# Moving the first batch's v from GpSimd's DMA queue to SyncE's in a fused attention and MLP-mixer kernel

## The chip, the cores and the metric

One core of a Trainium2 chip. The metric is device time in microseconds (us) of one execution; a profile of one execution gives the span. Where runs are timed in rounds, the kernel before runs on the same chip in the same rounds.

## The reference

```python
# q, k, v: (8 batches, 8 heads, 576, 64) float32; s: (8, 8, 576)
scores = scale * q @ k.T                       # causal
bias   = -(cum[:, :, :, None] - cum[:, :, None, :])   # cum = cumsum(max(s, 0))
attn   = softmax(where(causal, -1e9, scores + minimum(bias, 0)))
x      = (attn @ v) with the heads side by side          # (8, 576, 512)
u      = x + (relu(x.T @ w_tok1) @ w_tok2).T              # token mixing
out    = u + relu(u @ w_ch1) @ w_ch2                      # channel mixing
```

## The kernel before

A planner in the kernel simulates the engines with fixed durations and writes one static order of instructions for each engine, and that order is the program. k, q and the weights are cast to bf16 while loading, on GpSimd's queue. v stays float32. In the first batch its loads stand on GpSimd's queue too, between and behind k and q and ahead of the weights:

```python
def load(c=c, n=n, p0=p0):                     # chunk c of v: 128 positions, 8 heads
    (nc.sync if b >= 2 else nc.gpsimd).dma_start(
        out=vf.t[p0 : p0 + n, c, :, :],
        in_=v[b, :, c * 128 : c * 128 + n, :].rearrange("h p d -> p h d"))   # rows of 64 float32
...
# then on VectorE, chunk by chunk: vp = vf * wT   (all products with v need all five chunks)
...
sv = stage_v(0)
stage_qk(0, 0)                # first k and q
stage_qk(0, 1, (0,))          # second k
load_consts(); weights()
next(sv)                      # v, chunk 0
stage_qk(0, 1, (1,))          # second q
run(sv)                       # v, chunks 1 to 4
load_tok()                    # w1, w2, then wc1, v of batch 1, its k and q, wc2
```

Of k or q one load covers four of the eight heads, called a quad: 128 rows, each 4608 bytes of float32 read and 2304 of bf16 written. In idle stretches of the start the planner puts "unread matmuls" of zeros on TensorE to keep its clock up.

## Time and profile before

| | before |
|---|---|
| median of 5 runs | 288.22 us (287.94 to 288.91) |
| span of the profiled run | 289.3 us |
| TensorE busy | 278.7 us, 96% |
| last chunk of the first v multiplied, starts at | 19.48 us |
| first channel matmul (start of the dense part) | 28.7 us |

### The profile page before, as it was taken

To read this page: it belongs to the slowest core of one execution; us is meant where nothing else is said; L and a number is where in the kernel's file an instruction comes from. 1 tells how busy PE (TensorE), PEld (TensorE's weight loads), DVE (VectorE), ACT (ScalarE), POOL (GpSimd) and SP (SyncE) were. 2 spreads that over 40 slices of the span, in tenths; PEclk is the share of its full clock that TensorE was granted. 3 is DMA by queue.
4 is the path that set the end of the run, shared out by engine and by line. 5 is a ranking of instruction groups with operands and counts; after the bars stand their busy time and mean duration, and the time that the engine had idled before them with its cause. 6 is when DMAs were issued, how large, how long until landed. Compare 5 with 4: busy or idle time off the path is not lost.

```text
span 289.3 us, 6464 instructions
## 1 busy us (share of the span) xinstructions
PE 278.7 (96%) x2556; PEld 160.2 (55%) x2587; DVE 191.8 (66%) x425; ACT 169.2 (59%) x288; POOL 46.3 (16%) x97
## 2 busy tenths in 40 slices
PE   7799999999999999998999999999999999999994
PEld 2357866656664554455764454546764454457643
DVE  7756857899998998997986399889145360530022
ACT  4474787999975758744962269864770256107600
POOL 8775610121202021001100022200000000000000
PEclk9879999999999999999999999999999999999999
DMA  6999999999593999699383446893004410260032
GB/s 122 234 217 248 224 210 213 220 214 259 103 189 79 154 238 186 87 165 211 77 164 79 147 82 115 124 158 127 2 3 72 146 39 0 58 143 37 3 85 101
DMA packets 58483, 38.60 MB, mean 133 GB/s; under 512 B 44496, under 2 KB 48208, under 8 KB 58448
## 3 DMA queue, kind: packets, MB, share of 16 engines
q0 software_dynamic: 10128, 17.93, 35.6%
q1 hardware_dynamic: 48320, 20.21, 31.5%
q8 instruction: 21, 0.34, 0.5%
q14 instruction: 14, 0.11, 0.1%
HBM read 40.71 MB, written 9.44 MB: 173 GB/s over the span
## 4 chain that ended last, share of the span: by engine, by line
PE 89%; DVE 1%; issue 1%
PE pmx L952 33%; PE pmx L979 32%; PE psc L670 5%; PE pmx L813 5%; PE pmx L743 5%; PE pmx L883 4%; PE psc L813 1%; PE pmx L872 1%; PE pmx L839 1%; PE pmx L919 1%; DVE x L753 0%; DVE of L991 0%; PE pmx L1103 0%; PE pmx L984 0%; PE pmx L841 0%
## 5 line engine op out<-in xcount | busy, mean ns | idle before, releaser
L698 ACT ACTIVATE E<-psc 128x1024 bf16<-128x1024 f32 x62 | 60.3, 1021 | 40.7 <-PE psc L670 35.6
L952 PEld LDWEIGHTS <-wc 128*128 128x128 bf16 x624 | 59.5, 98 | 32.2 <-issue 1.7
L952 PE MATMUL pmx<-uTb,wc 128*128 128x320 bf16 x384 | 54.3, 299 | 0.8 <-DVE vp L570 0.8
L979 PE MATMUL pmx<-wc,gb 128*128 128x512 bf16 (+1 forms) x243 | 53.3, 369 | 0.4
L959 ACT ACTIVATE gb<-pmx 128x320 bf16<-128x320 f32 x75 | 32.0, 440 | 29.3 <-PE pmx L952 24.7
L598 ACT ACTIVATE junk<-qkn 128x1152 bf16<-128x1152 bf16 x32 | 37.2, 1163 | 11.8 <-DMA qkn<-in_q_dram 7.7
L979 PE MATMUL pmx<-wc,ga 128*128 128x512 bf16 x182 | 43.6, 379 | 0.5
L952 PE MATMUL pmx<-uTa,wc 128*128 128x512 bf16 (+1 forms) x234 | 43.4, 336 | 0.3
L979 PEld LDWEIGHTS <-gb 128*128 128x128 bf16 x252 | 24.1, 98 | 25.9 <-issue 0.7
L959 ACT ACTIVATE ga<-pmx 128x512 bf16<-128x512 f32 (+1 forms) x49 | 24.2, 503 | 9.6 <-PE pmx L952 7.2
L979 PEld LDWEIGHTS <-ga 128*128 128x128 bf16 x192 | 17.7, 98 | 20.6 <-issue 1.5
L706 DVE TENSOR_TENSOR E<-E,keep 128x512 bf16<-128x512 bf16 x58 | 23.7, 416 | 7.6 <-ACT E L698 7.4
L570 DVE TENSOR_TENSOR vp<-vf,wT 128x512 bf16<-128x512 f32 (+1 forms) x40 | 26.5, 681 | 1.0 <-DMA vf<-in_v_dram 0.9
L753 DVE TENSOR_TENSOR x<-pmx,rc 128x320 bf16<-128x320 f32 x60 | 26.9, 480 | 0.4
L670 PE MATMUL psc<-qT,kT 32*128 32x256 bf16 (+1 forms) x620 | 23.1, 255 | 2.1 <-DVE qT L642 1.5
L743 PEld LDWEIGHTS <-E 128*128 128x128 bf16 x576 | 21.0, 97 | 5.6 <-issue 0.7
L991 DVE TENSOR_TENSOR of<-pmx,ub 128x512 f32<-128x512 f32 (+1 forms) x17 | 11.2, 660 | 18.2 <-PE pmx L979 15.8
L670 PEld LDWEIGHTS <-kT 32*128 32x128 bf16 x640 | 14.7, 94 | 14.1 <-issue 11.5
L592 POOL DMA_DIRECT2D qkn<-in_k_dram x20 | 10.9, 543 | 69.7 <-DVE ga L961 26.9
L642 DVE STREAM_TRANSPOSE qT<-qkn 128x576 f32<-128x576 f32 x16 | 19.9, 1244 | 2.3 <-DMA qkn<-in_q_dram 2.3
L743 PE MATMUL pmx<-vp,E 128*128 128x65 bf16 x540 | 21.3, 193 | 0.0
L642 DVE STREAM_TRANSPOSE kT<-qkn 128x576 f32<-128x576 f32 x16 | 19.9, 1246 | 0.4 <-PE psc L670 0.4
(100 smaller groups left out, 230.4 us busy)
## 6 DMA issues: line engine op xcount, KB each, us to landing
out_dram<-of SPq DMA_DIRECT2D x31, 256.0 KB, 2.3
vf<-in_v_dram SPq DMA_DIRECT2D x24, 256.0 KB, 5.8
qkn<-in_k_dram POOLq DMA_DIRECT2D x20, 288.0 KB, 5.2
qkn<-in_q_dram POOLq DMA_DIRECT2D x20, 288.0 KB, 6.7
vf<-in_v_dram POOLq DMA_DIRECT2D x8, 256.0 KB, 8.7
wc<-in_moe_w_ch_dram POOLq DMA_DIRECT2D x4, 384.0 KB, 8.1
wc<-in_moe_w_ch_dram POOLq DMA_DIRECT2D x3, 512.0 KB, 12.0
out_dram<-of SPq DMA_DIRECT2D x10, 128.0 KB, 2.4
```

The costliest lines, as they stand in the source:

```text
L570: eng.tensor_tensor(out=vp.t[p0 : p0 + n, c, :, 0:D], in0=vf.t[p0 : p0 + n, c, :, :], in1=wT[p0 : p0 + n, cw, b * H : b * H + H].unsqueeze ...
L598: P.op({"ACT": (1.2, 1.6, lambda: nc.scalar.activation(out=junk[:, :], in_=n.t[:, :], func=AF.Square, accum_out=sq[:, col : col + 1]))}, r ...
L642: P.op({"DVE": (1.24, 1.4, lambda n=n, dst=dst: nc.vector.transpose(out=dst.t[:, 0:S, :].rearrange("d t e -> d (t e)").bitcast(FP32).rearr ...
L670: nc.tensor.matmul(out=pss[g // 2].bank(g % 2)[:, o], lhsT=kT.t[rows, j0 : j0 + 128, e], rhs=qT.t[rows, a:z, e], start=(e == 0 and not (fo ...
L698: nc.scalar.activation(out=E.t[:, :, gi * 512 : gi * 512 + 512], in_=ps.t[:, :, :], func=AF.Exp, scale=0.125)
L706: nc.vector.tensor_tensor(out=o, in0=o, in1=keep[:, :].unsqueeze(1).unsqueeze(1).to_broadcast([128, 2, 2, 128]), op=ALU.mult)
L743: nc.tensor.matmul(out=o[:, i, ic, 0 : D + 1], lhsT=E.t[:, hh, d0 : d0 + 128], rhs=vp.t[:, jc, h + hh, 0 : D + 1], start=(jc == j_lo), sto ...
L753: nc.vector.tensor_tensor(out=x.t[:, :, h0 * D : (h0 + n) * D].rearrange("p c (e d) -> p e c d", e=n), in0=view()[:, :, :, 0:D], in1=rc.t[ ...
L813: nc.tensor.matmul(out=pm()[:, (ha - h0) * D : (hb - h0) * D], lhsT=w1[:, NJ if odd and c == NJ - 1 else c, t * 128 : t * 128 + 128], rhs= ...
L952: nc.tensor.matmul(out=pm.t[:, 0 : e - a], lhsT=wc1[:, m, bass.ds(cc * 128, 128)], rhs=uT.t[:, m, a:e], start=(m == 0), stop=(m == NMC - 1))
L959: lambda cc=cc, pm=pm, a=a, e=e: nc.scalar.activation(out=g.t[:, cc, a:e], in_=pm.t[:, 0 : e - a], func=AF.Relu),
L979: nc.tensor.matmul(out=pm.t[:, 0 : d1 - d0], lhsT=g.t[:, cc, c * 128 : c * 128 + 128], rhs=wc2[:, cc, d0:d1], start=(cc == 0), stop=(cc == ...
```

## The change

Its intent: take v off GpSimd's queue, where its loads stand in front of the second q and of the weights, and let it come beside them on SyncE's queue once the first k is in: a tiny transfer that reads this k, called the gate, stands ahead of v's loads. With the move go new durations for the planner, a shorter fill of unread matmuls around the first scores, and stores of the last two batches in halves. The core of the diff:

```diff
-                (nc.sync if b >= 2 else nc.gpsimd).dma_start(
+                (nc.gpsimd if b == 1 else nc.sync).dma_start(
...
+            elif b == 0:
+                load_op(load, [(vf, c)], 1.5 * n / 128, True)      # planner: 1.5 us a chunk, beside the rest
...
-    sv = stage_v(0)
     stage_qk(0, 0)
     stage_qk(0, 1, (0,))
     load_consts()
     weights()
-    next(sv)
     stage_qk(0, 1, (1,))
-    run(sv)
+    n = qkn[(0, 0, 0)]
+    last[0] = P.op({"SP": (0.6, 0, lambda n=n: nc.sync.dma_start(out=gate[0:1, 8:16], in_=n.t[0:1, 0:8]))},
+                   reads=[(n, 0)], writes=["gate0"], prio=1, after=last[0])
+    run(stage_v(0))
     load_tok()
... (planner's durations: w1 2.2 -> 2.3, w2 1.9 -> 1.6, wc1 2.2 -> 1.95, wc2 2.6 -> 2.5, second k and q longer)
-        t0, t1 = rest[0], o.start - 0.12
+        t0, t1 = rest[0], o.start - (0.12 if len(rest) != 2 else 0.8)
...
-            t0 += n / 2400.0 * (2 if t0 < 5.0 else 1) + 0.003
+            t0 += n / 2400.0 * (2 if t0 < 6.2 else 1) + 0.003
... (output stores of the last two batches as two transfers of half the columns)
```

More of the change, by code (lines that the diff above doesn't have):

```diff
@@ L57, in __init__, with op @@
         self.readers = {}
-    def op(self, alts, reads=(), writes=(), prio=0, dma=0.0, holds=(), after=None, slow=0.0):
+    def op(self, alts, reads=(), writes=(), prio=0, dma=0.0, holds=(), after=None, slow=0.0, par=False):
         o = Op()
         o.slow = slow
+        o.par = par
         o.alts = alts
@@ L111, in run @@
         dma_free = 0.0
+        side_free = 0.0
         order = []
@@ L172, in run @@
             etime[e] = est + occ
-            if o.dma:
+            if o.par:
+                side_free = max(est + 1.3, side_free) + o.dma
+                fin = side_free + 0.6
+            elif o.dma:
                 s0 = max(est + (1.7 if e == "POOL" else 1.3), dma_free)
@@ L433, in load_p, with load_op @@
         lastp[0] = P.op({"POOL": (0.68 * n, 0, fn)}, writes=key, prio=1, dma=us, after=lastp[0])
-    def load_op(fn, key, us):
-        last[0] = P.op({"SP": (0.42, 0, fn)}, writes=key, prio=1, dma=us, after=last[0])
+    def load_op(fn, key, us, par=False):
+        last[0] = P.op({"SP": (0.42, 0, fn)}, writes=key, prio=1, dma=us, after=last[0], par=par)
     nc.vector.memset(zero[:, :], 0.0)
@@ L560, in stage_v @@
                 load_op(load, [(vf, c)], 1024 * 0.0226 / 16 * n / 128)
-            else:
-                load_p(load, [(vf, c)], (0.75 if b or c == 0 else 1.3) * n / 128, 1.4)
+            elif b == 0:
+                load_op(load, [(vf, c)], 1.5 * n / 128, True)
+            else:
+                load_p(load, [(vf, c)], 0.75 * n / 128, 1.4)
+            if b == 1:
                 yield
@@ L593, in load_quad @@
             out=n.t[:, :], in_=src[b, 4 * qd : 4 * qd + 4, :, :].rearrange("g (p r) d -> (g p) (r d)", r=R)),
-            [(n, 0)], 128 * 0.182 / 16)
+            [(n, 0)], 128 * (0.182 if b or qd == 0 else 0.3 if src is k else 0.36) / 16)
         return n
@@ L767, in load_tok @@
         load_w([(w1[:, 0:4, :], moe_w_tok1[0:512, :].rearrange("(c p) n -> p c n", p=128)),
-                (w1[0:64, 4, :], moe_w_tok1[512:576, :]), (w1[64:128, 5, :], moe_w_tok1[512:576, :])], "w1", 2.2)
+                (w1[0:64, 4, :], moe_w_tok1[512:576, :]), (w1[64:128, 5, :], moe_w_tok1[512:576, :])], "w1", 2.3)
         w = moe_w_tok2.rearrange("(c p) n -> p c n", p=128)
-        load_w([(w2[:, :, 0:S], w)], "w2", 1.9)
+        load_w([(w2[:, :, 0:S], w)], "w2", 1.6)
     def load_ch1(hf, m2):
@@ L775, in load_ch1 @@
                  moe_w_ch1[m2 * 256 : m2 * 256 + 256, c0 : c0 + DC // 2].rearrange("(m p) n -> p m n", p=128))],
-               ("wc1", hf, m2), 2.2)
+               ("wc1", hf, m2), 1.95)
     def load_ch2(g):
         load_w([(wc2[:, 4 * g : 4 * g + 4, :],
-                 moe_w_ch2[g * 512 : (g + 1) * 512, :].rearrange("(c p) n -> p c n", p=128))], ("wc2", g), 2.6)
+                 moe_w_ch2[g * 512 : (g + 1) * 512, :].rearrange("(c p) n -> p c n", p=128))], ("wc2", g), 2.5)
     hbuf = {}
@@ L1000, in st @@
                     if c < NJ - 1:
-                        nc.sync.dma_start(out=out[b, c * 128 : c * 128 + 128, d0:d1], in_=o.t[:, d0:d1])
+                        parts = 2 if (b == B - 1 and c < 3) or (b == B - 2 and c > 0) else 1
+                        for i in range(parts):
+                            w = (d1 - d0) // parts
+                            f0 = d0 + i * w
+                            nc.sync.dma_start(out=out[b, c * 128 : c * 128 + 128, f0 : f0 + w], in_=o.t[:, f0 : f0 + w])
                     else:
@@ L1105 @@
             fills.append(f)
-            t0 += n / 2400.0 * (2 if t0 < 5.0 else 1) + 0.003
+            t0 += n / 2400.0 * (2 if t0 < 6.2 else 1) + 0.003
         rest[0] = o.start + o.alts["PE"][0]
+        rest.append(o)
     order = sorted(order + fills, key=lambda o: (o.start, o.idx))
```

## The prediction

> **What bounds the kernel now.** I read the page first: busy shares, then the chain that ended last. Together they say that TensorE is the bound.
>
> ```profile
> PE 278.7 (96%) x2556; PEld 160.2 (55%) x2587; DVE 191.8 (66%) x425; ACT 169.2 (59%) x288; POOL 46.3 (16%) x97
> ...
> PE 89%; DVE 1%; issue 1%
> ```
>
> TensorE is busy 96% of 289.3 us. A change of loads can shorten only its idle time, its slow time and the work in it that nobody reads. So the second view is the busy time by stretch, cut where the start-up changes character.
>
> ```profile
> 0.00:5.00 5.00, 3.48 (x9) 1.28 (x10) 3.00 (x15) 2.18 (x5) 3.59 (x11) 1.00 0.51 97
> 5.00:11.50 6.50, 4.44 (x33) 2.00 (x30) 4.73 (x8) 1.29 (x3) 5.53 (x9) 1.00 1.08 229
> 11.50:18.00 6.50, 6.14 (x59) 2.87 (x59) 4.38 (x10) 4.13 (x5) 4.22 (x6) 0.51 1.22 200
> 18.00:23.20 5.20, 5.15 (x103) 3.63 (x105) 3.61 (x12) 3.84 (x5) 3.70 (x6) 0.95 1.15 234
> 23.20:285.80 262.60, 259.49 (x2358) 150.43 (x2386) 176.02 (x383) 157.80 (x271) 29.22 (x67) 1.00 0.65 129
> ```
>
> The columns after the length are busy us of PE, PEld, DVE, ACT, POOL, then the granted clock, the DMA share and GB/s. From 23.2 us on TensorE is busy 259.5 of 262.6 us at full clock: at most 3.1 us is idle there. The first 23.2 us are another regime: the DMA engines are full (share above 1), and between 11.5 and 18 us the granted clock is 0.51. What the change can win is therefore in the first 23.2 us, and the chain of waits by time indeed begins there, at 23.19 us. The third view is ScalarE's timeline of that start.
>
> ```profile
> 11.47 1.02 ACT L698 ACTIVATE E<-psc 128x1024 bf16<-128x1024 f32 x1 [3.47 <-PE psc L660]
> 12.93 1.09 ACT L695 ACTIVATE E<-pmx 128x512 bf16<-128x512 f32 x2 [0.43 <-PE pmx L670]
> 14.12 1.02 ACT L698 ACTIVATE E<-psc 128x1024 bf16<-128x1024 f32 x1
> 15.94 1.02 ACT L698 ACTIVATE E<-psc 128x1024 bf16<-128x1024 f32 x1 [0.80 <-PE psc L670]
> 18.01 1.02 ACT L698 ACTIVATE E<-psc 128x1024 bf16<-128x1024 f32 x1 [1.05 <-PE pmx L670]
> 18.93 1.08 ACT L695 ACTIVATE E<-pmx 128x512 bf16<-128x512 f32 x2
> 19.89 1.96 ACT L698 ACTIVATE E<-psc 128x1024 bf16<-128x1024 f32 x2
> ```
>
> These are the first batch's exponentials. They start at 11.47 and end at 21.85, so 10.38 us; the work in them is 6 x 1.02 + 1.09 + 1.08 = 8.3 us. About 2.1 us is waiting, all of it for scores. 1.6 us after the last one, at 23.43, the first token matmuls run and the dense part begins. The path of the start is: first k and q land, are transposed on VectorE, scores, eight rounds of exponentials, the last product with v, the division, token matmuls.
>
> The timeline of VectorE and TensorE shows where the 2.1 us come from.
>
> ```profile
> 8.95 1.26 DVE L642 STREAM_TRANSPOSE qT<-qkn 128x576 f32<-128x576 f32 x1 [1.74 <-DMA qkn<-in_q_dram]
> ...
> 12.59 1.19 DVE L642 STREAM_TRANSPOSE qT<-qkn 128x576 f32<-128x576 f32 x1
> ...
> 15.83 1.17 PE L1103 MATMUL pmx<-zero 128*128 128x512 bf16 x3
> ...
> 16.93 0.58 PEld L670 LDWEIGHTS <-kT 32*128 32x128 bf16 x16 [0.55 <-DVE vp L570]
> ```
>
> The second q is transposed by 13.78, yet the second quad's scores start at 16.93, just behind three unread matmuls (zeros, meant to keep the clock up) that at half clock took 1.17 us. ScalarE's wait of 1.05 us at 18.01 is their price. The planner put them there because its model has full clock and later operands.
>
> **What the Trainium skill says.** (1) "DMA: Bandwidth & Descriptors", section "Issuing engines are not separate DMA queues": loads issued from different engines run on the same 16 DMA engines and interleave; only issue time is saved. The trace agrees: the DMA share is already 1.08 to 1.22 from 5 to 23 us with nearly everything on GpSimd's queue, so a second queue adds no bandwidth. (2) Same page, "SWDGE vs HWDGE vs iDMA": a cast during the load must come from GpSimd. q, k and the weights land as bf16, v as float32, so v is the only one of them that can move. (3) "TensorE: Matmul & The Clock Gate", Part 1: the clock follows activity in windows of about 3.4 us, halved after idle ones. The trace agrees: TensorE stands from 8.8 to 10.26 waiting for q, and the clock is 0.50 from 12 to 18. (4) Same page, "Architectural detail": VectorE and ScalarE take their instructions strictly in order. So a multiply of a v that lands late also stops the transposes and masks queued behind it.
>
> **The change part by part.**
>
> *v of the first batch off GpSimd's queue.* In the trace GpSimd spends 1.14 us issuing v's first chunk at 3.83 and 3.40 us on the other four at 5.49; 4.54 us go. The second q is issued at 4.96 and should go at 4.96 - 1.14 = 3.8. The first piece of w1, now at 9.21, goes near 9.2 - 4.5 = 4.7. Counting its loads, GpSimd keeps at most eight unlanded: the eleventh waits at 10.58 for the third, the twelfth at 11.57 for the fourth. Without v the first eight are two k, two q, three pieces of w1 and w2, so weights are queued several us sooner. None of this is on the path by itself: w1 is first read at 23.2.
>
> *v on SyncE's queue.* A tiny transfer waits for the first k (landed by 5.97), costs about 0.6 us of issue (the same kind took 0.61 at 43.37), then five loads at about 0.5 us each (median 0.544 for SyncE's v loads): issued from 6.6 to 9.1. They must land before the products with v, which start at 20.39 now. Landing takes a median of 5.8 us for SyncE's loads of v, so about 12.5 to 16. Before, the last was multiplied at 19.48. Enough slack, so being beside the others is no gain in itself.
>
> *The contention.* The 1.2 MB of v now share the DMA engines with the end of the first q and with the second k and q. First q: it lands at 8.95, v's first packets move around 8; I charge +0.3 us, straight on the path. Second k and q: before, one chunk of v lay between them, so of the v traffic 256 KB came ahead of the second q; now perhaps two or three chunks do. Against that stands the issue 1.1 us sooner. The second q lands about 12.5 now; I expect 13 to 13.5, transposed by 14.7. The four exponentials of quad zero end at 16.96, so this stays off the path.
>
> *Fewer unread matmuls.* The fill stops 0.8 instead of 0.12 us ahead of the first scores and counts them at half clock until 6.2 us. That shortens a block of six (7.42 to 8.77, 1.35 us) that lay in front of a wait until 10.26: worth nothing there, and it may leave the clock low a little longer. But the new load times also move the gaps that the planner sees. I expect most of the block at 15.83 to go (-0.9 of the 1.05), and of the two at 22.04 (0.55 us, between the last exponential at 21.85 and the last product at 22.42) about half (-0.3). For the 0.80 and 0.43 us waits of quad zero I take -0.3, as the masks and scores are less mixed with v's multiplies.
>
> *The stores in halves.* Each extra store costs SyncE about 0.36 us (median of its output stores). Those of the last batch issue from 278.37 to 286.2, 2.6 us apart; the last pair is in halves already. What follows the last matmul is unchanged: the addition, 0.42 us from 285.39, and a landing of about 2.4 us. Those of the batch before come behind the transposes through DMA (257.91 against 256.60), so they delay none. Two of VectorE's additions wait for output buffers (3.8 us together after 225 us), but TensorE does not. I take 0 to -0.1.
>
> *Sum.* +0.3 - 0.9 - 0.3 - 0.3 - 0.1 = -1.3 us in the start and tail; in the long middle 0, with a scatter of about 1 us because the whole static order is planned anew. 288.84 - 1.3 = 287.5; I say 287.4.
>
> **The rivals.** *Nothing comes of it:* a later first q and a colder clock eat what the unread matmuls gave. For it: the start is limited by DMA, and the bytes are the same. That gives 288.5 to 289. *v lands late and blocks VectorE:* 256-byte rows of v take turns with rows of 4.6 KB of k and q; if v comes at 15 to 18, its multiplies stop masks and divisions queued behind them and the products with v start after 20.4. For it: VectorE already waited 0.47 and 0.39 us for v at 15.10 and 16.18. That gives 289.5 to 290.5. *The start wins its whole slack:* exponentials back to back from 11.47 end at 19.8, 2.1 us sooner, and the new order also removes the later stall at 132 us (VectorE on the path for 2.4 us there); 285 to 286. Against it: the clock is half in exactly those microseconds, and scores of one round then take about as long as its exponential.
>
> **Range and chances.** The start can give at most about 2 us, the middle's whole idle time is 3.1 us, and 2% is 5.8 us, which would need both and more. A loss of 5.8 us would need a stall longer than any in the trace's dense part. So: 287.4 us, 285.7 to 289.3 in 8 of 10; faster by over 2% 0.03, within 2% 0.95, slower 0.02.
>
> **What would show it.** Right: v's loads on SyncE's queue from about 6.6 us; w1's first piece issued near 4.7; the second quad's scores before 16 with no block of unread matmuls just ahead; exponentials ending near 20.5 instead of 21.85; token matmuls from about 22 instead of 23.43, and after that the same length as now to within 1 us. Wrong: the first q's transpose much after 9.3; multiplies of v with waits on loads above 1 us; exponentials ending at 21.5 or later; or a start that wins while the rest from the token matmuls to the last addition grows or shrinks by more than 1 us, so that the planner's new order and not the loads decides.

## More of the kernel before

The kernel before ranged from 287.05 to 292.13 us over all its runs here (the run of 292.13 is classed as slow and left out of ratios), so a few us between single runs mean nothing.

One chunk of v is 1024 rows of 256 bytes (the fifth is half of that), the whole v of a batch 4608 rows.

The prediction shows most of the page. What it does not show are the totals of the DMA queues (packets, MB, share of the 16 engines) and two rows of the list of issues, whose last column is the median us from issue to landing:

```profile
q0 software_dynamic: 10128, 17.93, 35.6%
q1 hardware_dynamic: 48320, 20.21, 31.5%
...
vf<-in_v_dram SPq DMA_DIRECT2D x24, 256.0 KB, 5.8
...
vf<-in_v_dram POOLq DMA_DIRECT2D x8, 256.0 KB, 8.7
```

q0 is GpSimd's queue, q1 SyncE's. The bytes are alike, the packets are not: 1770 bytes in a mean packet of q0, 418 in one of q1.

## The result and the profile after

The changed kernel takes 321.49 us (median of 5 runs, 321.01 to 322.99) against 288.22 us. The ratio is 1.1153, 95% interval 1.1121 to 1.1186. The kernel is 33 us slower, and the result is correct.

Line numbers shift between kernels: the multiply of v is L570 before and L577 here, the channel matmuls L952 and L959. First the same two lines of the page, then the chain of waits up to 48 us (start, length, what):

```profile
PE 280.5 (88%) x2552; PEld 161.4 (50%) x2583; DVE 191.0 (60%) x427; ACT 167.8 (52%) x286; POOL 41.1 (13%) x92
...
PE 78%; DMA 9%; SPq 6%; ACT 3%; issue 2%; DVE 1%; ACTq 0%; POOLq 0%
```

```profile
6.65 0.43 SPq L561
...
7.13 0.68 SPq L561
...
7.85 7.55 SPq L561
...
15.44 9.51 SPq L561
...
25.00 22.97 DMA vf<-in_v_dram
...
47.99 0.69 DVE vp L577
```

TensorE does the same work (280.5 us busy against 278.7) in a longer span. The chain now begins with v. L561 is SyncE issuing v's five loads: the first two issues take 0.43 and 0.68 us, the next two 7.55 and 9.51 us, the fifth ends at 34.4 us, and its load lands 22.97 us after its issue began. VectorE's timeline shows what waits for it:

```profile
19.63 0.69 DVE L577 TENSOR_TENSOR vp<-vf,wT 128x512 bf16<-128x512 f32 x1 [8.41 <-DMA vf<-in_v_dram]
29.34 0.69 DVE L577 TENSOR_TENSOR vp<-vf,wT 128x512 bf16<-128x512 f32 x1 [9.02 <-DMA vf<-in_v_dram]
29.95 1.25 DVE L649 STREAM_TRANSPOSE qT<-qkn 128x576 f32<-128x576 f32 x1
...
37.83 0.69 DVE L577 TENSOR_TENSOR vp<-vf,wT 128x512 bf16<-128x512 f32 x1 [6.63 <-DMA vf<-in_v_dram]
...
45.00 0.69 DVE L577 TENSOR_TENSOR vp<-vf,wT 128x512 bf16<-128x512 f32 x1 [6.48 <-DMA vf<-in_v_dram]
...
47.99 0.68 DVE L577 TENSOR_TENSOR vp<-vf,wT 64x512 bf16<-64x512 f32 x1 [2.29 <-DMA vf<-in_v_dram]
```

The four full chunks come 7 to 10 us apart, the half one 3 us later, and the waits add up to 32.8 us. The last multiply starts at 47.99 instead of 19.48. The second q, landed by 11 us, is transposed only at 29.95 because two multiplies stand ahead of it on VectorE. The busy time by stretch (columns as in the prediction) shows the hole on TensorE:

```profile
11.50:18.00 6.50, 2.64 (x25) 1.22 (x24) 0.00 (x0) 2.69 (x4) 3.36 (x5) 0.94 1.20 201
18.00:23.20 5.20, 0.00 (x0) 0.00 (x0) 0.69 (x1) 0.00 (x0) 2.17 (x3) 0.50 1.13 253
23.20:60.00 36.80, 15.11 (x172) 10.51 (x175) 11.36 (x24) 6.82 (x14) 5.32 (x11) 0.57 0.97 176
```

From 18 to 23.2 us TensorE does nothing; from 23.2 to 60 it is busy 15.1 of 36.8 us, at a granted clock of 0.57. Meanwhile the DMA share is 0.97 to 1.20: the DMA engines are full all the time, with something else. The dense part starts at 60.5 instead of 28.7 us, 31.8 us later. From there to the end it is 320.1 - 60.5 = 259.6 us, against 289.3 - 28.7 = 260.6. All of the loss is in the start.

What the DMA engines did instead of v is in the packets of each queue by stretch. These are 12 to 16 us, 16 to 20 us and, last line alone, 48 to 52 us:

```profile
q0 software_dynamic: 582, 0.65, 93.2%
q1 hardware_dynamic: 579, 0.15, 27.1%
...
q0 software_dynamic: 471, 0.82, 94.3%
q1 hardware_dynamic: 469, 0.12, 20.6%
...
q1 hardware_dynamic: 3796, 0.96, 128.3%
```

While both queues have work, the engines serve as many packets of one as of the other: 582 and 579, 471 and 469. The counts stay equal within 3 packets in every stretch of 4 us from 12 to 44 us, in which GpSimd's queue took 92 to 95% of the engines' time. They are not equal before: v's first packets move only near 10 us, and from 8 to 12 us the counts are 777 and 294. But a packet of GpSimd's queue carries 1.1 to 1.7 KB here and one of SyncE's 256 bytes. At 48 to 52 us GpSimd's queue moves nothing, and SyncE's queue does 3796 packets in 4 us, eight times its rate between 16 and 20. The totals of the queues give v's packets:

```profile
q0 software_dynamic: 9760, 16.75, 31.2%
q1 hardware_dynamic: 53888, 21.39, 30.4%
```

GpSimd's queue has 10128 - 9760 = 368 packets fewer. So on GpSimd's queue the 4608 rows of this v travelled in 368 packets, 12.5 rows each on average; on SyncE's they are about 4600 packets (an experiment below shows exactly one per row). The same bytes need 12.5 times as many turns.

### The profile page after: what moved, and what is told of

Same layout as the page of the kernel before. It is cut to its first block, busy times and chain, and to the rows that moved or that the text cites. A ratio compares the mean times of both kernels' runs of the same rounds, so it can differ in the third digit from the quotient of the medians.

```text
span 320.1 us, 6466 instructions
## 1 busy us (share of the span) xinstructions
PE 280.5 (88%) x2552; PEld 161.4 (50%) x2583; DVE 191.0 (60%) x427; ACT 167.8 (52%) x286; POOL 41.1 (13%) x92
## 3 DMA queue, kind: packets, MB, share of 16 engines
q0 software_dynamic: 9760, 16.75, 31.2%
## 4 chain that ended last, share of the span: by engine, by line
PE 78%; DMA 9%; SPq 6%; ACT 3%; issue 2%; DVE 1%; ACTq 0%; POOLq 0%
PE pmx L986 28%; PE pmx L959 28%; DMA vf<-in_v_dram 7%; SPq L561 6%; PE psc L677 5%; PE pmx L820 5%; PE pmx L750 5%; PE pmx L890 4%; DMA qkn<-in_k_dram 1%; ACT E L705 1%; ACT junk L605 1%; DMA uTb<-us 1%; PE pmx L879 1%; PE psc L820 1%; PE psc L750 1%
## 5 line engine op out<-in xcount | busy, mean ns | idle before, releaser
L959 PEld LDWEIGHTS <-wc 128*128 128x128 bf16 x624 | 59.1, 98 | 31.7 <-issue 1.3
L959 PE MATMUL pmx<-uTb,wc 128*128 128x320 bf16 x384 | 54.5, 299 | 0.1
L577 DVE TENSOR_TENSOR vp<-vf,wT 128x512 bf16<-128x512 f32 (+1 forms) x40 | 26.2, 681 | 33.0 <-DMA vf<-in_v_dram 32.8
L959 PE MATMUL pmx<-uTa,wc 128*128 128x512 bf16 (+1 forms) x234 | 43.9, 336 | 0.4
L677 PE MATMUL psc<-qT,kT 32*128 32x256 bf16 (+2 forms) x620 | 23.3, 256 | 18.6 <-DVE qT L649 17.8
L750 PE MATMUL pmx<-vp,E 128*128 128x65 bf16 x540 | 22.6, 196 | 13.6 <-DVE vp L577 13.2
L750 PEld LDWEIGHTS <-E 128*128 128x128 bf16 x576 | 22.8, 101 | 19.3 <-issue 12.6
L966 ACT ACTIVATE ga<-pmx 128x512 bf16<-128x512 f32 (+1 forms) x45 | 22.1, 511 | 15.6 <-PE pmx L959 13.4
L760 DVE TENSOR_TENSOR x<-pmx,rc 128x320 bf16<-128x320 f32 x60 | 26.6, 478 | 0.2
L998 DVE TENSOR_TENSOR of<-pmx,ua 128x512 f32<-128x512 f32 x12 | 8.3, 691 | 24.0 <-PE pmx L986 22.1
L998 DVE TENSOR_TENSOR of<-pmx,ub 128x512 f32<-128x512 f32 (+1 forms) x17 | 11.2, 658 | 16.7 <-PE pmx L986 12.9
```

The lines of the kernel that those rows point to most:

```text
L577: eng.tensor_tensor(out=vp.t[p0 : p0 + n, c, :, 0:D], in0=vf.t[p0 : p0 + n, c, :, :], in1=wT[p0 : p0 + n, cw, b * H : b * H + H].unsqueeze ...
L677: nc.tensor.matmul(out=pss[g // 2].bank(g % 2)[:, o], lhsT=kT.t[rows, j0 : j0 + 128, e], rhs=qT.t[rows, a:z, e], start=(e == 0 and not (fo ...
L750: nc.tensor.matmul(out=o[:, i, ic, 0 : D + 1], lhsT=E.t[:, hh, d0 : d0 + 128], rhs=vp.t[:, jc, h + hh, 0 : D + 1], start=(jc == j_lo), sto ...
L760: nc.vector.tensor_tensor(out=x.t[:, :, h0 * D : (h0 + n) * D].rearrange("p c (e d) -> p e c d", e=n), in0=view()[:, :, :, 0:D], in1=rc.t[ ...
L959: nc.tensor.matmul(out=pm.t[:, 0 : e - a], lhsT=wc1[:, m, bass.ds(cc * 128, 128)], rhs=uT.t[:, m, a:e], start=(m == 0), stop=(m == NMC - 1))
L966: lambda cc=cc, pm=pm, a=a, e=e: nc.scalar.activation(out=g.t[:, cc, a:e], in_=pm.t[:, 0 : e - a], func=AF.Relu),
```

## The experiments

**The theories.** *Q, turns:* the DMA engines take packets from the two queues in turn, one for one; v on SyncE's queue is 4608 small packets and gets one turn for each packet of GpSimd's queue until that runs dry. *S:* SyncE's queue moves 256-byte rows slowly by itself. *B:* the queues share by bytes or by a fixed priority. *G:* the late start behind the first k costs. *H:* the in-order engines, blocked behind early multiplies, cost. *O:* the other parts of the change, or the planner's new order, cost.

All kernels below also write the never-taken fallback branch with copies ahead of its matmuls; the changed kernel itself does not. The control asks whether that moves anything:

> Control: the changed kernel with only the never-taken fallback branch written with copies ahead of its matmuls, as all kernels of these experiments have it. Both theories: 319 to 323 us; anything else would mean that the edit itself moves the time.

Measured, single run: 321.83 us, last multiply of v at 48.69, dense part from 60.1 us. As expected.

**Only v moved, nothing else of the change** (the kernel before plus the move, the gate and the planner's 1.5 us a chunk):

> The kernel before with only the first batch's v moved to SyncE's queue behind the first k; unread matmuls, stores and weight costs as before. Theory Q: 317 to 324 us, last multiply of v near 48 us, packets of the two queues equal in number in every stretch between 12 and 44 us. Rival O: 288 to 291 us.

Measured: 320.13 us (319.98 to 320.9), ratio 1.1089, interval 1.0996 to 1.1183. Last multiply of v at 47.71. The move alone makes 31.7 of the 33 us, so the other parts of the change aren't needed for the loss; the order that the planner makes of the move is in this run too, and the runs with larger rows below judge it. The expected equal counts came, within 3%, in every stretch of 4 us from 12 to 44 us but one: from 28 to 32 us they are 354 and 551. There GpSimd's queue ran low, 54 packets and 71% of the engines' time from 29 to 30 us, and SyncE's served 216; from 30 to 31, with GpSimd's at 95%, they are 81 and 81 again.

**v put back, the rest of the change kept** (only the planner's durations for v and for the second k and q go back with it):

```diff
-                (nc.gpsimd if b == 1 else nc.sync).dma_start(
+                (nc.sync if b >= 2 else nc.gpsimd).dma_start(      # and the loads' order as before
```

> The changed kernel with only the first batch's v put back on GpSimd's queue as before; the reworked unread matmuls, the stores in halves and the planner's new weight costs stay. Theory Q (the loss is v's packets on SyncE's queue taking turns one for one with GpSimd's packets): 286 to 290 us, no wait of a v multiply above 1 us, dense part from about 28 to 29 us. Rival O (the replanned order, fewer unread matmuls or the halved stores cost the 32 us): stays near 320 us.

Measured: 298.8 us (298.17 to 299.08), ratio 1.0341, interval 1.0253 to 1.0428. A miss for both: the last multiply of v is back at 20.35 us and the start at 30.5, but 10 us remain. They are mostly not in the start: from the dense part to the end it is 297.2 - 30.5 = 266.7 us, 6.1 more than before. The chain of this kernel at 71 to 79 us:

```profile
71.00 1.00 issue
72.00 0.24 ACT junk L608
72.24 1.83 ACT E L708 x2
74.07 0.74 ACT junk L608
...
77.04 1.14 ACT junk L608 x2
78.18 0.34 ACT gb L969
```

L608 are ScalarE's squares for an overflow check that no product waits for; the planner's new order has them between exponentials that TensorE waits for. TensorE is busy 18.05 of 20 us from 70 to 90 here, 19.89 before. Next run: the planner's weight durations set back as well, which restores ScalarE's order of before and leaves the shorter fill and the halved stores.

```diff
-                ... "w1", 2.3)   ... "w2", 1.6)   ... ("wc1", hf, m2), 1.95)   ... ("wc2", g), 2.5)
+                ... "w1", 2.2)   ... "w2", 1.9)   ... ("wc1", hf, m2), 2.2)    ... ("wc2", g), 2.6)
```

> The kernel with the first v back on GpSimd's queue as above, and the planner's durations of the weights also set back, so that ScalarE's order is that of the kernel before; what stays of the change is the shorter fill of unread matmuls and the stores in halves. If the 10 us that remained with v put back come from the planner's new order (weights' durations): 286 to 290 us. If they come from the fill or the halved stores: 295 us or more.

Measured: 292.4 us (289.74 to 294.28), beside 289.74 of before (287.05 to 291.08): ratio 1.0058, interval 0.9914 to 1.0201. One of its four runs, 294.28, is classed as slow and is not in the ratio. The median lies between the two forecasts, but the interval includes no change, and dense part to end is 290.5 - 29.1 = 261.4 us. So fill and stores are worth nothing that these runs can show (the interval allows up to 2%, 5.8 us), and most of the 10 us came from four numbers in the planner's model: between the two runs the ratio falls from 1.0341 to 1.0058. In the changed kernel the same squares stand on its chain at 99 to 105 us, but its dense part was no longer than before.

**GpSimd's weights held until v has landed.** One small copy on GpSimd that reads all five chunks, ahead of w1 and everything behind it:

```diff
     run(stage_v(0))
+    lastp[0] = P.op({"POOL": (0.2, 0.3, lambda f=vfs[0]: nc.gpsimd.tensor_copy(out=gate[0:1, 1:6], in_=f.t[0:1, :, 0, 0]))},
+                    reads=[(vfs[0], c) for c in range(NJ)], writes=["gate1"], prio=1, after=lastp[0])
     load_tok()
```

> The changed kernel, but GpSimd's queue waits with w1 and everything behind it until all five chunks of the first v have landed. Theory Q: once the second q has landed (about 11 us) SyncE's queue has the DMA engines alone and runs at the 950 packets a us seen at 48 to 52 us, so the remaining 4300 packets take 4.5 us and the last v lands at 15 to 17 us; total 285 to 290 us. Rival S (SyncE's queue moves rows of 256 bytes slowly by itself, about 140 packets a us, whatever the other queue does): v still lands after 38 us and the total is above 320 us, since the weights come later still.

Measured: 294.14 us (292.57 to 295.73), ratio 1.0165, interval 1.0065 to 1.0266; 27 us of the loss gone. SyncE's queue alone from 12 to 14 us, and the copy that marks v's landing:

```profile
q1 hardware_dynamic: 1273, 0.32, 70.4%
...
16.68 0.35 POOL L1040 CAST gate<-vf 1x5 bf16<-1x5 f32 x1 [7.16 <-DMA vf<-in_v_dram]
```

Same rows, same queue: 1273 packets in 2 us instead of 469 in 4, and v has landed by 16.7 us. S falls, and so does most of H, since the multiplies stood as early as ever. The rate from 12 to 16 us is 640 to 720 packets a us, not the 950 that was assumed from a later stretch, but v landed in time. The total is 4 us above its range of 285 to 290; the chain has six unread matmuls (16.88, 2.47 us) ahead of the second quad's scores. Same hold in the kernel of before:

> The kernel before with the first v on SyncE's queue and GpSimd's weights held until it has landed, all else as before (the run with only v moved took 320.1 us). Theory Q: the last v lands at 15 to 17 us as in the held kernel, so 288 to 296 us, the spread being the planner's order. Rival S or O: 315 us or more.

Measured: 292.97 us (291.78 to 294.29), ratio 1.0116, interval 1.0009 to 1.0223, against 320.13 without the hold. The last two multiplies of v run from 15.2 us. As expected.

**The same hold without unread matmuls after 10 us:**

```diff
-    WARM = 95.0
+    WARM = 10.0
```

> The held kernel (GpSimd's weights wait until the first v has landed) with no unread matmuls planned after 10 us; its trace had six of them (2.4 us) in front of the second quad's scores, on the chain. If they cost what the chain says: dense part 2 us sooner, at 29 to 30 us instead of 31.4, total 290 to 293 us instead of 294.1. If the colder clock takes it back: 293 to 296 us.

Measured: 294.45 us (293.82 to 294.76), ratio 1.0163. The dense part starts at 26.6 us, 4.8 sooner than with the hold alone and 2.1 sooner than before, yet nothing is won. The total lies in the range forecast for a colder clock, but by luck: the granted clock from 14 to 18 us was 0.77, against 0.50 with the hold alone. The wait that took the place of the gain, in the list of TensorE's waits (total us, times, longest):

```profile
PE pmx L967 <- DMA wc<-in_moe_w_ch_dram: 3.5, 2, 2.9
```

The weights that were held back now arrive late for the channel matmuls; in the changed kernel and before TensorE never waits for them. With dense part to end at 293.1 - 26.6 = 266.5 us, the start's gain is given back.

**Fewer, larger rows.** The same bytes into the same buffers by the same five loads, read as contiguous rows. Wrong values:

```diff
+                if b == 0:
+                    flat = v[b].rearrange("h s d -> (h s d)")[c * 65536 : c * 65536 + n * 512]
+                    nc.sync.dma_start(out=vf.t[0:n, c, :, :].rearrange("p h d -> p (h d)").rearrange("p (x e) -> p x e", e=512),
+                                      in_=flat.rearrange("(x p e) -> p x e", p=n, e=512))      # e=128 for rows of 512 bytes
+                    return
```

> The changed kernel with the first v read in contiguous rows of 2 KB into the same buffers, same bytes, same five loads, one eighth of the packets (576 instead of 4608); the values land in wrong places, so the result is wrong on purpose. Theory Q: 576 packets at about 145 a us are through in 4 us, the last v lands at 12 to 15 us; total 285.5 to 289 us. Rival B (each queue gets a fixed share of bytes, or SyncE's queue the lower priority): v lands as late as now, total near 320 us.

Measured: 291.18 us (289.14 to 292.77), ratio 1.0099, interval 0.9998 to 1.02; result wrong. Above the range of Q and 30 us off B. The planner's input, and with it the static order of every engine, is that of the changed kernel, so neither that order nor the in-order engines make the loss by themselves: O and H fall here too. The last multiply of v starts at 17.36; v was expected at 12 to 15. SyncE's queue has 49856 packets, 4032 fewer than the changed kernel: exactly 4608 - 576, so one packet per row. (Each transfer adds a few packets of its own: with only v moved SyncE's total is 4704 above that of before, 4608 rows and 96 more for six new transfers, 16 each. If GpSimd's transfers have 16 too, which no run shows, the 368 packets of v there were 288 with 16 rows each, an estimate from these counts.)

> The changed kernel with the first v read in contiguous rows of 512 bytes: same bytes, half the packets (2304); the values land in wrong places, wrong on purpose. Theory Q counts turns: GpSimd's queue had given about 2200 turns by 28 us in the changed kernel, so the last v lands at 27 to 31 us, and with the 12 us that the changed kernel takes from the last v to the dense part the total is 298 to 304 us, between the 321 us of 256-byte rows and the 289 to 293 us of 2 KB rows. Rival B (share by bytes or by priority, with 2 KB rows fast for another reason): 315 us or more.

Measured, single run: 308.44 us; last multiply of v at 34.72, dense part from 46.8. Between the two, as only counting turns says, but v came 4 us later than the range of 27 to 31, and the total is 4 us above its range. 51584 packets: 2304 fewer, again one per row. The packets of the two queues, first with 2 KB rows from 12 to 14 us, then with 512-byte rows from 16 to 20:

```profile
q0 software_dynamic: 208, 0.20, 58.8%
q1 hardware_dynamic: 203, 0.37, 55.7%
```

```profile
q0 software_dynamic: 432, 0.76, 88.2%
q1 hardware_dynamic: 432, 0.21, 25.5%
```

Turns are equal again, whatever the bytes: with 2 KB rows v takes nearly twice the bytes of the other queue, with 512-byte rows a quarter, with 256-byte rows a seventh (0.12 to 0.82 MB). B falls. Part of the miss of 4 us is the rate: I took the turns of the changed kernel, 424 per 4 us at 20 to 24; with larger packets of v between them there were 396, and by 28 us v had 2071 turns instead of some 2200. The rest is the tail, where turns were no longer equal: from 28 to 32 us 357 to 299, from 32 to 36 us 664 to 30. Why stays open.

**v begun at once, without the gate:**

> The changed kernel without the small transfer that lets v begin only after the first k, so v's loads are issued from about 1.7 us. Theory Q: v gets some 400 to 500 turns more during the loads of k and q, and the last v lands 3 to 5 us earlier, at 43 to 45 us; total 316 to 319 us; the gate is not the cause. Rival G (the late start of v is what costs): below 310 us.

Measured, single run: 316.31 us. The total is as expected, its working is not: the last v was multiplied at 37.56 instead of 43 to 45 us, so the early turns were worth 10 us of landing. They were more than one for one: from 4 to 6 us SyncE's queue served 966 packets and GpSimd's, with 56% of the engines' time, 101; from 10 to 12 us, with GpSimd's at 88%, they are 370 and 368. The gain reached the end only in part, as the planner had put the second k's and q's transposes behind multiplies of v (the second q's at 34.42), and the dense part began 16.8 us after the last v instead of 12.5. G falls as the main cause, as the total is not below 310; beginning late does cost.

**The planner told the truth about v:**

```diff
-                load_op(load, [(vf, c)], 1.5 * n / 128, True)
+                load_op(load, [(vf, c)], (11.0 if c == 0 else 8.5) * n / 128, True)
```

> The changed kernel with only the planner's duration of the five loads of the first v set to about what the trace shows (11 us for the first chunk, 8.5 us for the others, instead of 1.5), so that the static order puts the second q's transpose, the second quad's scores and exponentials ahead of the multiplies with v. Theory Q: the loads are as slow as before, the last v lands at 42 to 48 us and the products with v still wait for it; the total falls by 2 to 6 us, to 315 to 319 us. Rival H (the in-order engines blocked behind early multiplies are the main cost): below 305 us.

Measured, single run: 327.82 us, 6 slower instead of 2 to 6 faster. The second q is transposed at 12.13 and its scores and exponentials are done long before v, but the planner filled the long wait:

```profile
39.66 15.21 PE L1121 MATMUL pmx<-zero 128*128 128x512 bf16 x68
```

The view begins near 40 us and shows 68 unread matmuls; seen from 12 us on, the block begins at 22.38 and has 147. It ends at 54.9, 3 us after the last v's multiply, which runs from 51.26; v itself was expected at 42 to 48. H falls as the main cause, but with a flaw that a last run had to remove: the same without unread matmuls after 10 us.

> The told kernel (planner given the long durations of the first v) without unread matmuls after 10 us. Its trace had 68 of them between 39.7 and 54.9 us, while the last v was multiplied by 51.9, so they held the products with v back by about 2.8 us. Theory Q: the last v still lands at 47 to 52 us and the total is 322 to 326 us instead of 327.8. Rival H (in-order engines behind early multiplies are the main cost, and only the unread matmuls hid it): below 310 us.

Measured, single run: 328.21 us, another miss in size: the last v is multiplied at 49.83, as expected, and the products with v begin at 50.57 now, but TensorE then waits 3.35 us for exponentials on ScalarE, where squares are queued, and the dense part starts at 65.3. H's forecast of below 310 us is out of reach: with every other engine ahead of v, v still lands near 50 us and the loss stays. No kernel tried here with a right result beats the kernel before.

| run | rows of v on SyncE's queue | last multiply of v, us | dense part, us | span, us |
|---|---|---|---|---|
| before | 0 | 19.48 | 28.7 | 289.3 |
| changed | 4608 of 256 B | 47.99 | 60.5 | 320.1 |
| rows of 512 B | 2304 | 34.72 | 46.8 | 306.8 |
| rows of 2 KB | 576 | 17.36 | 27.1 | 287.6 |
| weights held | 4608 of 256 B | 16.9 | 31.4 | 294.1 |

## Why the prediction was wrong

**The step that failed** is "Landing takes a median of 5.8 us for SyncE's loads of v, so about 12.5 to 16". The loads landed 12.9 to 30.0 us after issue and v was complete at 48. The 5.8 us were measured on later batches, where the same rows are loaded while GpSimd's queue leaves room: from 60 to 80 us before, it took 56% of the engines' time with 977 packets, and SyncE's queue had 4644. In the changed kernel it took 92 to 95% from 12 to 44 us. The figure was carried from one state of the queues to another. A count of turns was at hand: before, GpSimd's queue served 352 packets from 4 to 8 us and 809 from 12 to 16, so 88 to 200 a us, and 4608 turns at such rates are 23 to 52 us. Begun at 7 us, that estimate ends between 30 and 59. The term before it, "five loads at about 0.5 us each", failed with it: the five issues ran from 6.65 to 34.4 us. The prediction's own sign of being wrong, "multiplies of v with waits on loads above 1 us", is what VectorE's timeline shows.

**The sum.** The last v is 28.5 us later than before (47.99 less 19.48). From it to the dense part it took 12.5 us instead of 9.2, as the second quad's last scores were still to do and the clock was low; 3.3 more. Together 31.8, less 1.0 us of a slightly shorter dense part, gives the 30.8 us between the spans.

**The rival that came true** was named: "v lands late and blocks VectorE", with the right mechanism, small rows taking turns with large ones. It was sized at v coming "at 15 to 18" and a loss of about 1 us, without counting the rows. Slower by over 2% got a chance of 0.02 because "a loss of 5.8 us would need a stall longer than any in the trace's dense part"; the stall was in the start, where the prediction itself had said that another regime reigns.

**The Trainium skill.** The prediction rightly took from "DMA: Bandwidth & Descriptors", "Issuing engines are not separate DMA queues", that a second queue adds no bandwidth, and read from it that it does no harm. The same page, section "Queues, rings and completion order", says that each DMA engine goes round the queues and drains a whole packet of one before it switches. The runs agree where GpSimd's queue kept the engines busy (above 90% of their time from 12 to 44 us): equal counts. Where it left room, SyncE's served more (966 to 101, above). With packets of unequal size that rule explains the lateness of v, and the prediction had not applied it. On the clock the prediction says that its trace agrees with the page; the trace doesn't show that. TensorE's wait from 8.8 to 10.26 is 1.5 us, under half of the window of 3.4, and the clock was still 1.00 from 10 to 11 us and 0.83 from 11 to 12, when TensorE was busy again.

**The other terms.** GpSimd's issue moved as worked out: the second q at 3.83 and w1 from 4.37 us. The first q was not later by 0.3 us; its transpose was at 7.76 instead of 8.95. But this varies without pattern (7.1 to 9.4 us over these kernels, 9.41 with only v moved, whose GpSimd queue is the same); why stays open. Unread matmuls: the block ahead of the second scores became six at 12.95, and nothing waited for them. Their worth cannot be read from this kernel; with v and the weights' durations put back, fill and stores together are inside the spread. The halved stores cost nothing visible: from the last batch's channel matmuls to the end it is 30.3 us after and 30.1 before. The middle kept its length within 1 us in the changed kernel, as forecast, but that was luck of the order: with v put back it was 6 us longer.

## What to carry to other kernels

Before moving a load to a second DMA queue, count the packets it becomes there and the packets of the queue that it will run beside: engines that alternate packets gave a queue of 256-byte rows a seventh of the other's bytes (0.12 to 0.82 MB from 16 to 20 us) for as long as the other kept them busy. A landing time measured where the other queue leaves room says nothing of a full one. And after a change to a planner's numbers, look at the whole static order again: four small durations made most of 10 us here.

## What the Trainium skill lacked or had wrong

- "DMA: Bandwidth & Descriptors" gives about 9 to 17 descriptors as typical of a packet. On GpSimd's queue that fits, on average (4608 rows of v in 368 packets, 12.5 each); on SyncE's queue each row was a packet of its own (4032 packets fewer when 4608 rows became 576).
- The same page says that spreading loads over issuing engines doesn't help. It lacks that it can hurt: here the same 1.2 MB took from 6.6 to 48 us beside GpSimd's loads, and to 16.7 us with those held, and the kernel lost 33 us.
- No page that I read gives how far SyncE's issue runs ahead: with 256-byte rows the third and fourth loads blocked it for 7.55 and 9.51 us, with 2 KB rows none took over 0.55 us.
